# Rebuilding 64-bit weights from rows that are loaded one byte late, and products of zeros in TensorE's modelled idle time

## The chip, the cores and the metric

The kernel runs on one core of a Trainium2 chip. The metric is the time of one execution on the device in microseconds (us); three runs of the kernel before took 1581.19 to 1584.06 us, median 1582.57. The engines of a core run side by side and wait for each other by semaphores: TensorE (PE; PEld is its weight load), VectorE (DVE), ScalarE (ACT), GpSimd (POOL) and SyncE (SP), whose queue issues all the DMAs here. Each engine takes its instructions in program order.

## The reference

Three layers over 8 sequences of 576 tokens (4608 tokens, 512 features): a landmark attention (8 heads of 64), a layer with a Fourier mix, a normalization and two matrices, and a gated layer with three matrices.

```python
A, Bm, C = sm(q, k_lm), sm(q_lm, k_lm), sm(q_lm, k)      # softmaxes; 32 landmarks
Z = Bm.T / (norm1(Bm) * norminf(Bm) + 1e-06)
for _ in range(6):
    Z = 2 * Z - Z @ Bm @ Z
x = heads_to_features(A @ Z @ C @ v)                      # 8 x 576 x 512
u = x + real(fft(fft(x, axis=1), axis=2))
un = (u - mean(u)) / sqrt(var(u) + 1e-06)
x = u + relu(un @ w_ch1) @ w_ch2                          # 512 x 2048, 2048 x 512
xk, xr = mu_k * x + (1 - mu_k) * x_prev, mu_r * x + (1 - mu_r) * x_prev
k = relu(xk @ w_k)                                        # 512 x 1024
out = sigmoid(xr @ w_r) * ((k * k) @ w_v)                 # 512 x 512, 1024 x 512
```

The five matrices arrive as 64-bit floats. The kernel makes a 32-bit float of each value and splits it in two 16-bit floats, high and low part; a product of two matrices is then three matmuls (high by high, high by low, low by high).

## The kernel before, in words

**Stages.** `phase1` does the attention and the Fourier mix of one sequence (batch) at a time, in 32-bit floats, and adds its result to blocks `ub` of 512 tokens. `norm` normalizes such a block: sums by matmuls with a column of ones (`one`), three Newton steps on small tiles, then the two halves `un`. `block_a` multiplies it with w_ch1 and w_ch2: 16 steps `first(f)` (12 matmuls into a bank `ph`, then Relu on ACT and the low part on DVE) and 16 steps `second(f)` (12 matmuls into the four banks `acc`), 384 matmuls of 128x512 for a block. There are nine blocks; after the last comes the gated layer (`Gated`), 280 us behind the start and later mostly matmuls back to back. The matmuls of `block_a` and `Gated` form one chain in fixed order.

**Weights.** `Weights.run` handles a piece of 128x512 weights: 32 pieces of w_ch1 and w_ch2 (in the order four of w_ch1, four of w_ch2, four times), then 20 pieces of the gated layer, whose halves go back to memory. A piece is loaded as pairs of 32-bit words (512 KB) into one of three rooms in turn (`wst` twice, `more`; the last eight of the 32 pieces use `wst` alone). Then come three ACT passes (Square, Sign and Copy make a mask of the exponent), three DVE passes on integers (shifts, and, or), an ACT pass for the high half (`w1h`, `w2h`) and a DVE pass for the low half (`w1l`, `w2l`). The room is free for the next load when the low half is done. `first(0)` needs the first four pieces, `second(f)` the f-th of w_ch2.

**What sets the order.** All operations are recorded first; `Plan.issue` is a list scheduler that gives each engine its order by modelled costs: an operation can stand as soon as its inputs' modelled ends plus HOP (0.2) have passed, and among those ready the one with the highest key (longest way to the end, plus a lead: NOW for the chain, START for the first batch, SOON for the others, CONVERT for weights) goes first. Weight operations get a further margin `slack` on each edge from another engine or a DMA, 1.5 in the kernel before. A DMA is modelled with its bytes / 340e3 plus 2.0. PSUM has eight banks: `acc` holds 0 to 3, `ph` 4 and 5, and banks from `gp()` take any that are free, all eight as long as the chain hasn't begun.

**Names.** Line 180 is the helper that issues every operation of DVE, ACT and POOL, L308 every DMA, L323 every matmul, L336 every transpose by TensorE; groups are told apart by tile names. `kbd`, `qbd`: landmarks of keys and queries; `RX`, `bdR`: the six steps of the series for Z; `Ae`, `Ao`, `acs`: the Fourier tables' products; `tmp`: squares for the variance; `small`: the Newton steps; `h`: the inner activations.

Of the kernel before, what the change touches and what calls it, by code (L numbers as in the profile page):

```python
# [11 lines left out]
F32 = mybir.dt.float32  # L12
F16 = mybir.dt.float16
I32 = mybir.dt.int32
AF = mybir.ActivationFunctionType
ALU = mybir.AluOpType
AX = mybir.AxisListType
# [13 lines left out]
WCH = 512  # L31
# [96 lines left out]
class Op:  # L128
    def __init__(self, index, eng, run, cost, port=False, nbytes=0):
        self.index, self.eng, self.run, self.cost = index, eng, run, cost  # L130
        self.port, self.nbytes = port, nbytes
        self.preds, self.succs = set(), []
        self.tail = self.lead = self.est = self.end = 0.0
        self.group = self.last = None

NOW, START, CONVERT, SOON = 1000.0, 400.0, 170.0, 200.0


class Engine:
# [44 lines left out]
class Plan:  # L187
# [6 lines left out]
    def __init__(self, nc, shadow):  # L194
        self.nc, self.shadow = nc, shadow
        self.ops, self.groups = [], []
        self.slots, self.turn = {}, {}
        self.lead = self.slack = 0.0
        self.chained, self.count = None, 0
        self.v = Engine(self, nc.vector, "v")  # L200
        self.s = Engine(self, nc.scalar, "s")
        self.g = Engine(self, nc.gpsimd, "g")
# [112 lines left out]
    def mm(self, out, lhsT, rhs, start, stop, chain=False, **kw):  # L315

        cost = wide(rhs) / 2400.0 + 0.0025
        if rhs.dtype == F32:
            cost = max(4 * cost, 0.17)
        share = 4 if wide(lhsT) <= 32 else 2 if wide(lhsT) <= 64 else 1  # L320

        def run():
            self.nc.tensor.matmul(  # L323
                out.real(), lhsT=lhsT.real(), rhs=rhs.real(), start=start, stop=stop, **kw
            )

        op = self.record("pe", run, cost / share, [out], [lhsT, rhs])
        if chain:
            op.lead = 0.0
            if self.chained:  # L330
                op.preds.add(self.chained)
            self.chained = op

    def tr(self, out, in_, ident):
        def run():
# [29 lines left out]
    def issue(self):  # L365
        ops = self.ops
# [17 lines left out]
        avail = {e: [] for e in free}  # L384
        pending, order = [], []
        bank = {n: 0.0 for n in range(8)}
        fixed, holds = set(), {}
        port = dma = 0.0

        def ready(op):  # L390
            op.est = max(
# [48 lines left out]
        for op in ops:  # L440
            if not op.preds:
                ready(op)
        while len(order) < sum(op.eng is not None for op in ops):
            when = []
            for e in free:
                if avail[e]:
                    when.append((free[e], e))
                elif later[e]:
                    when.append((max(free[e], later[e][0][0]), e))
            g = grant()  # L450
            if g and (not when or g[0] <= min(when)[0]):
                t, op, got = g
                pending.remove(op)
                for x, b in zip(op.group, got):
                    x.bank, x.left = b, len(x.ops)
# [10 lines left out]
            start = max(t, port) if op.port else t  # L466
            free[e] = end = start + op.cost
# [5 lines left out]
            op.begin = start  # L473
            order.append(op)
            done(op, end)
        self.order, self.span = order, max(op.end for op in order)
        for op in order:
            op.run()
# [18 lines left out]
class Weights:  # L497


    KEEP = float(np.int32(0x3FFFFFFF).view(np.float32))  # L500

    def __init__(self, iss, pool):
        self.iss, self.pool = iss, pool

    def run(self, src, hi, lo, room=None):


        iss = self.iss
        v_, s_ = iss.v, iss.s
        st, bits = room or (  # L510
            iss.tile(self.pool, [128, WCH, 2], I32, "wst", bufs=2),
            iss.tile(self.pool, [128, WCH], I32, "wbits", bufs=2),
        )
        iss.load(st.rearrange("p f w -> p (f w)"), src)
        low, high = st[:, :, 0], st[:, :, 1]


        w = bits.bitcast(F32)
        s_.activation(bits, high.bitcast(F32), AF.Square, scale=256.0)
        s_.activation(w, bits, AF.Sign)  # L520
        s_.activation(w, w, AF.Copy, scale=self.KEEP)
        v_.scalar_tensor_tensor(
            bits, high, 3, bits, op0=ALU.logical_shift_left, op1=ALU.bitwise_and
        )
        v_.scalar_tensor_tensor(
            bits, low, 29, bits, op0=ALU.logical_shift_right, op1=ALU.bitwise_or
        )
        v_.scalar_tensor_tensor(
            bits, high, -0x40000000, bits, op0=ALU.bitwise_and, op1=ALU.bitwise_or
        )  # L530
        dram = None
        if hi is None:
            dram = lo
            both = st.rearrange("p f w -> p (f w)")[:, 0:WCH].bitcast(F16).rearrange(
                "p (x f) -> p x f", x=2
            )
# [419 lines left out]
def build(nc, tc, a):  # L956
# [5 lines left out]
    with stack, tc.manual_schedule():  # L962
# [30 lines left out]
        one = iss.tile(com, [128, 1], F32, "one")  # L993
        v_.memset(one, 1.0 / DM)
        ones = one.to_broadcast([128, 128])
        w1 = [iss.tile(pa, [128, 4, FF1], F16, f"w1{x}") for x in "hl"]
        w2 = [iss.tile(pa, [128, 16, DM], F16, f"w2{x}") for x in "hl"]
        weights = Weights(iss, com)
# [128 lines left out]
        def block_a(i, un):  # L1127
            u = ub[i]
            acc = acc_banks()
            hs = {}  # L1130
            iss.lead = NOW

            def first(f):
                ps = ph()
                sl = slice(128 * f, 128 * f + 128)
                for c in range(4):
                    for n, (x, y) in enumerate(PARTS):
                        mm(
                            ps, w1[x][:, c, sl], un[c][y], c == 0 and n == 0,
                            c == 3 and n == 2, chain=True,  # L1140
                        )
                h = hs[f] = iss.tile(com, [128, 2, 512], F16, "h", bufs=3)
                s_.activation(h[:, 0], ps, AF.Relu)
                v_.scalar_tensor_tensor(
                    h[:, 1], ps, 0.0, h[:, 0], op0=ALU.max, op1=ALU.subtract
                )

            def second(f):
                h = hs.pop(f)
                for m in range(4):  # L1150
                    sl = slice(128 * m, 128 * m + 128)
                    for n, (x, y) in enumerate(PARTS):
                        mm(
                            acc[m], w2[x][:, f, sl], h[:, y], f == 0 and n == 0,
                            f == 15 and n == 2, chain=True,
                        )

            first(0)
# [10 lines left out]

        more = iss.place(pa, [128, 4 * BLK], I32, "more", "ub_2")  # L1170
        rooms = [None, None, (
            more[:, 0:2 * WCH].rearrange("p (f w) -> p f w", w=2), more[:, 2 * WCH:3 * WCH]
        )]
        iss.lead, iss.slack = CONVERT, 1.5
        for n, x in enumerate(w12_items):
            weights.run(*x, room=rooms[n % 3] if n < 24 else None)
        iss.lead = 0.0
# [247 lines left out]
```

## Time and profile before

| | |
|---|---|
| median of three runs | 1582.57 us |
| profiled execution: time, span | 1584.5 us, 1582.7 us |
| busy over the span | PE 1529.7, DVE 883.9, ACT 600.5, POOL 288.4 us |
| granted TensorE clock, mean | 0.978 of full |
| DVE: 156 integer passes on weights (132 + 24) | 94.4 + 16.8 us |

The busy time of PE adds up matmuls whose ends are modelled; the granted clock (PEclk) says what share of 2.4 GHz the chip allowed, 0.50 being 1.2 GHz. Rows of a timeline or of groups name the operation as out<-in with sizes; "x40" counts records, and a 32-bit matmul leaves two of them.

### The profile page before, as it was taken

How to read it: one execution, taken by the hardware profiler on the slowest of the kernel's cores; microseconds unless marked ns; L12 is line 12 of the kernel's file. 1: busy time of each engine (PE TensorE's matmuls, PEld its weight loads, DVE VectorE, ACT ScalarE, POOL GpSimd, SP SyncE). 2: the span in 40 equal slices, each digit the busy share in tenths (PEclk: the TensorE clock that was granted, in tenths of full speed). 3: DMA queues.
4: the chain of work that ended last, by engine and by line, in shares of the span. 5: the costliest groups of instructions: out<-in, count | busy, mean ns of one | idle time of the engine just before them, and what ended most of it. 6: DMA issues, size and time to landing. Idle time of an engine off the chain costs nothing.

```text
span 1582.7 us, 20918 instructions
## 1 busy us (share of the span) xinstructions
PE 1529.7 (97%) x8182; PEld 784.4 (50%) x8182; DVE 883.9 (56%) x1802; ACT 600.5 (38%) x1233; POOL 288.4 (18%) x347
## 2 busy tenths in 40 slices
PE   6879899999999999999999999999999999999998
PEld 5535455555564554554544444444444444444443
DVE  6798887776764764634515344211587766643222
ACT  4465654444433433322312123111655544443221
POOL 2012020221210210210102012000454533221100
PEclk8788899999999999999999999999999999999999
DMA  7243414132322222100002200000121011000000
GB/s 272 67 133 121 134 55 152 38 115 76 100 71 81 86 72 80 61 1 28 1 0 80 107 28 0 27 0 28 53 80 54 27 54 54 28 1 27 27 28 27
DMA packets 43587, 97.87 MB, mean 62 GB/s; under 512 B 4064, under 2 KB 9440, under 8 KB 42976
## 3 DMA queue, kind: packets, MB, share of 16 engines
q1 hardware_dynamic: 43488, 96.53, 17.8%
q8 instruction: 65, 1.06, 0.3%
q14 instruction: 34, 0.28, 0.1%
HBM read 72.39 MB, written 24.12 MB: 61 GB/s over the span
## 4 chain that ended last, share of the span: by engine, by line
PE 93%; DVE 4%; ACT 1%; issue 1%; DMA 0%; SPq 0%; POOL 0%; ACTq 0%; DVEq 0%
PE ph L323 35%; PE acc L323 35%; PE gp L323 21%; PE gp L336 2%; DVE wbits L180 1%; DVE more L180 0%; DVE small L180 0%; DMA k<-in_k 0%; DVE uc L180 0%; DVE w1l L180 0%; DVE h L180 0%; ACT h L180 0%; DVE d L180 0%; DVE un L180 0%; DVE w2l L180 0%
## 5 line engine op out<-in xcount | busy, mean ns | idle before, releaser
L323 PE MATMUL ph<-un,w1h 128*128 128x512 f16 x1152 | 353.6, 382 | 10.6 <-DVE bst L180 6.1
L323 PE MATMUL acc<-h,w2h 128*128 128x512 f16 x1152 | 350.8, 382 | 1.2 <-ACT w2h L180 1.2
L180 DVE SCALAR_TENSOR_TENSOR h<-ph,h 128x512 f16<-128x512 f32 x144 | 99.3, 690 | 283.2 <-ACT h L180 282.4
L180 ACT ACTIVATE h<-ph 128x512 f16<-128x512 f32 x144 | 85.9, 597 | 379.2 <-PE ph L323 378.7
L323 PE MATMUL acc<-h,w2l 128*128 128x512 f16 x576 | 219.8, 382 | 4.3 <-DVE w2l L180 4.3
L323 PE MATMUL ph<-un,w1l 128*128 128x512 f16 x576 | 219.8, 382 | 3.1 <-DVE w1l L180 3.1
L323 PE MATMUL ph<-xk,w_k 128*128 128x512 f16 x864 | 199.6, 379 | 0.0
L323 PE MATMUL acc<-w_v,k 128*128 128x512 f16 x864 | 198.9, 379 | 0.0
L323 PEld LDWEIGHTS <-w1h 128*128 128x128 f16 x1152 | 113.0, 99 | 138.4 <-issue 14.5
L323 PEld LDWEIGHTS <-w2h 128*128 128x128 f16 x1152 | 113.6, 99 | 131.6 <-issue 8.8
L180 DVE TENSOR_TENSOR rk<-rk 128x512 f32<-128x512 f32 x72 | 55.5, 770 | 146.3 <-ACT rk L180 145.9
L323 PEld LDWEIGHTS <-k 128*128 128x128 f16 x864 | 84.6, 98 | 100.6
L323 PEld LDWEIGHTS <-w_k 128*128 128x128 f16 x864 | 84.5, 98 | 99.7
L323 PE MATMUL gp<-w_r,xr 128*128 128x512 f16 x432 | 99.3, 379 | 0.7 <-ACT rs L180 0.7
L180 DVE SCALAR_TENSOR_TENSOR wbits<-wst,wbits 128x512 int32<-128x512 int32 x132 | 94.4, 731 | 2.8 <-ACT wbits L180 1.6
L180 ACT ACTIVATE rk<-ph 128x512 f32<-128x512 f32 x72 | 43.0, 597 | 129.2 <-PE ph L323 121.6
L323 PEld LDWEIGHTS <-w2l 128*128 128x128 f16 x576 | 57.1, 99 | 69.9 <-DVE w2l L180 5.3
L323 PEld LDWEIGHTS <-w1l 128*128 128x128 f16 x576 | 57.1, 99 | 68.6 <-DVE w1l L180 4.6
L180 DVE TENSOR_TENSOR k<-rk,k 128x512 f16<-128x512 f32 x72 | 59.3, 823 | 29.3 <-ACT k L180 29.1
L180 POOL TENSOR_TENSOR sq<-sq 128x513 f32<-128x513 f32 x27 | 36.6, 1356 | 198.7 <-ACT sq L180 198.1
L180 POOL TENSOR_TENSOR xr<-xt,xr 128x512 f16<-128x512 f32 x36 | 48.6, 1375 | 112.1 <-ACT xr L180 112.0
L323 PEld LDWEIGHTS <-xr 128*128 128x128 f16 x432 | 42.2, 98 | 51.4 <-issue 0.9
(156 smaller groups left out, 1977.3 us busy)
## 6 DMA issues: line engine op xcount, KB each, us to landing
wst<-in_w_ch SPq DMA_DIRECT2D x24, 512.0 KB, 4.0
q<-in_q SPq DMA_DIRECT2D x16, 578.0 KB, 5.1
k<-in_k SPq DMA_DIRECT2D x16, 576.0 KB, 4.6
ys<-ub SPq DMA_DIRECT2D x36, 256.0 KB, 2.1
out<-o SPq DMA_DIRECT2D x36, 256.0 KB, 2.0
yb<-ys SPq DMA_DIRECT2D x8, 1026.0 KB, 5.3
v<-in_v SPq DMA_DIRECT2D x8, 1024.0 KB, 5.6
more<-in_w_ch SPq DMA_DIRECT2D x8, 512.0 KB, 4.4
```

What stands on the lines that cost most here:

```text
L180: f(real(out), *map(real, args), **{k: real(x) for k, x in kw.items()})
L323: self.nc.tensor.matmul(out.real(), lhsT=lhsT.real(), rhs=rhs.real(), start=start, stop=stop, **kw)
L336: self.nc.tensor.transpose(out.real(), in_.real(), ident.real())
```

## The change

**The load.** A row of 512 values (4096 bytes) is written to its room from byte 1 on, so that a value's top byte (sign and upper exponent bits) lies alone at the start of the next word pair and the following four bytes of interest form one aligned word. Two Prelu on ACT turn the signed top byte into the top byte of the 32-bit float and write it into `top`, a tile that was set to zero once; one DVE pass shifts the word right by 5 and ors `top` in, in place. The high and low halves then read that word with a stride of 8 bytes. The pieces of the gated layer use one `top` (the other's place holds their halves).

**Products of zeros.** Where the planner's model leaves TensorE idle, `issue` puts int((idle - 0.15) / 0.3) matmuls of a zero tile (128x128 by 128x512) in front of the next matmul: before the chain into bank 3, which no other tile then uses, and inside a block's chain into `acc[3]`, adding zero. There are 102 of them: 28 in front of the first matmul, 89 ahead of the chain's first, 13 later in the first block.

**The margin.** `slack` for weight operations goes from 1.5 to 0.6.

```diff
-    KEEP = float(np.int32(0x3FFFFFFF).view(np.float32))
+    EDGE, STEEP = 56.125, 1024.0
...
-        iss.load(st.rearrange("p f w -> p (f w)"), src)
-        low, high = st[:, :, 0], st[:, :, 1]
-        w = bits.bitcast(F32)
-        s_.activation(bits, high.bitcast(F32), AF.Square, scale=256.0)
-        s_.activation(w, bits, AF.Sign)
-        s_.activation(w, w, AF.Copy, scale=self.KEEP)
+        iss.load(st.bitcast(U8)[:, 1:8 * WCH + 1], src.bitcast(U8))
+        def words(dt, at):
+            return st.bitcast(dt)[:, at:2 * WCH + at].rearrange("p (f w) -> p f w", w=2)[:, :, 0]
+        x = words(F32, 2)
+        byte = st.bitcast(I8)[:, 8:8 * WCH + 8].rearrange("p (f b) -> p f b", b=8)[:, :, 0]
+        s_.activation(x, byte, AF.Prelu, bias=self.EDGE, alpha=self.STEEP)
+        s_.activation(
+            top.bitcast(I8).rearrange("p (f b) -> p f b", b=4)[:, :, 3], x, AF.Prelu,
+            scale=8.0, bias=-8.0 * (56.0 + self.EDGE), alpha=1.0 / self.STEEP,
+        )
         v_.scalar_tensor_tensor(
-            bits, high, 3, bits, op0=ALU.logical_shift_left, op1=ALU.bitwise_and
+            words(I32, 1), words(I32, 1), 5, top,
+            op0=ALU.logical_shift_right, op1=ALU.bitwise_or,
         )
-        v_.scalar_tensor_tensor(
-            bits, low, 29, bits, op0=ALU.logical_shift_right, op1=ALU.bitwise_or
-        )
-        v_.scalar_tensor_tensor(
-            bits, high, -0x40000000, bits, op0=ALU.bitwise_and, op1=ALU.bitwise_or
-        )
+        w = words(F32, 1)
...
-        fixed, holds = set(), {}
+        fixed, holds = {WARM}, {}
...
+            if e == "pe" and (not warming or warming[-1] is not None):
+                into = warming[-1] if warming else None
+                idle = start - max(was, self.warm_from.end)
+                order += [
+                    Op(0, "warm", partial(self.warm, into), 0.0)
+                ] * int((idle - 0.15) / 0.3)
...
+            z = zero.real()[:, 0:1]
+            nc.tensor.matmul(
+                into.real() if into else spare[0], lhsT=z.to_broadcast([128, 128]),
+                rhs=z.to_broadcast([128, 512]), start=not into, stop=not into,
+            )
...
-        iss.lead, iss.slack = CONVERT, 1.5
+        iss.lead, iss.slack = CONVERT, 0.6
```

DVE at the end of the first batch's series, where the first pieces are converted (`wbits`, `more`, `wst`: rooms and masks; `bdY`: end of the series; `ks`, `qs`: the second batch's landmarks). Before:

```order
L180 TENSOR_TENSOR RX1_305<-gp_441,RX1_305 128x64
L180 SCALAR_TENSOR_TENSOR wbits_272<-wst_108,wbits_272 128x512
L180 SCALAR_TENSOR_TENSOR bdY_465<-gp_452,bst_187,c_mask4_92 128x256 x2
...
L180 SCALAR_TENSOR_TENSOR wbits_312<-wst_110,wbits_312 128x512 x3
L180 SCALAR_TENSOR_TENSOR more_112<-more_112 128x512 x3
L180 SCALAR_TENSOR_TENSOR w1l_529<-wbits_272,w1h_505 128x512
L180 TENSOR_REDUCE ks_534<-k_176 128x32
```

The same place now:

```order
L186 TENSOR_TENSOR RX1_349<-gp_495,RX1_349 128x64
L186 SCALAR_TENSOR_TENSOR w1l_505<-wst_116,w1h_476 128x512
L186 SCALAR_TENSOR_TENSOR bdY_518<-gp_507,bst_223,c_mask4_100 128x256 x2
L186 SCALAR_TENSOR_TENSOR wst_118<-wst_118,wtop_84 128x512
L186 SCALAR_TENSOR_TENSOR more_86<-more_86 128x512
L186 TENSOR_REDUCE ks_549<-k_212 128x32 x3
L186 SCALAR_TENSOR_TENSOR w1l_505<-wst_118,w1h_476 128x512
```

Three integer passes for a piece have become one, the first low half stands ahead of `bdY` rather than behind three pieces' passes, and the second batch's landmarks follow sooner.

PE at the chain's first matmul (`ph`), behind the first block's variance (`one`,`tmp`) and the transposes that spread its result (`ident`,`small`). Before:

```order
L323 MATMUL gp_629<-one_80,tmp_627 128x1 x4
L323 MATMUL gp_629<-one_80,tmp_638 128x1 x4
L336 MATMUL gp_677<-ident_90,small_661 128x128 x4
L323 LDWEIGHTS w1h_505
L323 MATMUL ph_706<-un_687,w1h_505 128x512
```

The same place now (`E_747` is the second batch's; of the 11 products of zeros in front of the chain one is shown, and one of the 6 in front of the transposes of `E_747`):

```order
L330 MATMUL gp_798<-one_82,tmp_808 128x1 x4
L346 MATMUL gp_843<-ident_98,E_747 128x128
...
L1043 LDWEIGHTS zero_88
L1043 MATMUL spare_125<-zero_88 128x512
...
L346 MATMUL gp_843<-ident_98,E_747 128x128 x3
...
L346 MATMUL gp_868<-ident_98,small_837 128x128 x4
...
L330 LDWEIGHTS w1h_476
L330 MATMUL ph_903<-un_883,w1h_476 128x512
```

46 matmuls of the second batch's attention, and the products of zeros, now stand ahead of the chain's first matmul (247 others instead of 201).

ACT around the same place (`un`: high halves of the normalized block; `h`: first inner activation). Before:

```order
L180 ACTIVATE un_694<-uc_620 128x512
L180 ACTIVATE wbits_698<-wst_659 128x512
L180 ACTIVATE wbits_698<-wbits_698 128x512 x2
L180 ACTIVATE un_708<-uc_623 128x512
L180 ACTIVATE h_728<-ph_706 128x512
```

The same place now:

```order
L186 ACTIVATE un_888<-uc_786 128x512
L186 ACTIVATE un_905<-uc_794 128x512
L186 ACTIVATE w1h_476<-wst_759 128x512
L186 ACTIVATE wst_877<-wst_877 128x512
L186 ACTIVATE wtop_84<-wst_877 128x512
L186 ACTIVATE h_931<-ph_903 128x512
```

The four high halves stand together; weight passes of the ninth and later pieces lie between them and `h`.

## Rows read from the trace of the kernel before

**Rows 1.** The page: span of the profiled execution.
```profile
span 1582.7 us, 20918 instructions
```

**Rows 2.** Five stretches: stretch, length, then busy us and instructions by engine.
```profile
core 0: us, PE busy (x) PEld busy (x) DVE busy (x) ACT busy (x) POOL busy (x), PEclk, DMA share, GB/s
0.00:82.20 82.20, 59.41 (x336) 43.87 (x337) 56.35 (x147) 37.78 (x91) 10.69 (x19) 0.77 0.47 163
82.20:120.00 37.80, 28.18 (x157) 14.41 (x157) 34.55 (x67) 22.26 (x41) 4.57 (x5) 0.91 0.47 148
120.00:280.00 160.00, 146.60 (x897) 80.75 (x898) 126.08 (x284) 87.63 (x200) 23.02 (x29) 0.93 0.34 112
280.00:1574.00 1294.00, 1291.54 (x6776) 643.78 (x6775) 664.15 (x1303) 452.86 (x905) 250.08 (x294) 1.00 0.13 46
1574.00:1582.70 8.70, 3.94 (x19) 1.57 (x16) 2.82 (x4) 0.00 (x0) 0.00 (x0) 0.85 0.32 121
```

**Rows 3.** Order of time on PE: start, length, what, idle before and its releaser.
```profile
9.07 6.80 PE L323 MATMUL gp<-kbd,q 128*97 128x64 f32 x40 [9.07 <-POOL kbd L180]
...
67.45 6.46 PE L323 MATMUL gp<-one,tmp 128*128 128x1 f32 x32 [1.52 <-ACT tmp L180]
...
82.22 1.01 PE L323 MATMUL ph<-un,w1h 128*128 128x512 f16 x2 [4.47 <-ACT wbits L180]
83.03 0.63 PE L323 MATMUL ph<-un,w1l 128*128 128x512 f16 x1
83.46 1.06 PE L323 MATMUL ph<-un,w1h 128*128 128x512 f16 x2
...
89.25 0.38 PE L323 MATMUL acc<-h,w2l 128*128 128x512 f16 x1
89.47 0.59 PE L323 MATMUL acc<-h,w2h 128*128 128x512 f16 x2
...
93.78 2.88 PE L323 MATMUL gp<-kbd,q 128*97 128x64 f32 x32
...
224.84 3.63 PE L323 MATMUL gp<-one,tmp 128*128 128x1 f32 x32
```

**Rows 4.** A stretch of the first batch, same columns as Rows 2.
```profile
24.00:52.00 28.00, 24.73 (x181) 18.22 (x179) 20.82 (x65) 14.96 (x43) 8.73 (x13) 0.58 0.42 142
```

**Rows 5.** SP in order of time: loads into the room `more`.
```profile
88.98 0.33 SPq L308 DMA_DIRECT2D more<-in_w_ch  x1
...
179.90 0.34 SPq L308 DMA_DIRECT2D more<-in_w_ch  x1
```

**Rows 6.** Groups by shape: busy us, mean ns, idle before and its releaser.
```profile
L180 DVE SCALAR_TENSOR_TENSOR wbits<-wst,wbits 128x512 int32<-128x512 int32 x132 | 94.4, 731 | 2.8 <-ACT wbits L180 1.6
L180 ACT ACTIVATE wbits<-wst 128x512 int32<-128x512 f32 x44 | 29.2, 663 | 1.8 <-DVE w2l L180 1.4 <-ACT w2h L180 0.4
L180 ACT ACTIVATE wbits<-wbits 128x512 f32<-128x512 int32 x44 | 27.5, 627 | 0.9
L180 POOL TENSOR_TENSOR tmp<-tmp 128x512 f32<-128x512 f32 x21 | 27.2, 1295 | 74.4 <-ACT tmp L180 73.9
L180 POOL MEMSET xt<- 128x1 f32 x64 | 5.1, 98 | 29.1 <-ACT xt L180 29.0
```

**Rows 7.** Instructions on the tile `wst` by stretch: DVE busy, ACT busy, clock, DMA.
```profile
82.20:120.00 37.80, 12.79 (x18) 3.32 (x5) 0.91 0.47 148
120.00:280.00 160.00, 37.32 (x50) 11.22 (x17) 0.93 0.34 112
```

**Rows 8.** DMA issues: count, KB each, median us from issue to landing.
```profile
wst<-in_w_ch SPq DMA_DIRECT2D x24, 512.0 KB, 4.0
ys<-ub SPq DMA_DIRECT2D x36, 256.0 KB, 2.1
yb<-ys SPq DMA_DIRECT2D x8, 1026.0 KB, 5.3
v<-in_v SPq DMA_DIRECT2D x8, 1024.0 KB, 5.6
```

More of the change, by code (lines that the diff above doesn't have):

```diff
@@ L14 @@
 I32 = mybir.dt.int32
+I8 = mybir.dt.int8
+U8 = mybir.dt.uint8
 AF = mybir.ActivationFunctionType
@@ L133, in __init__ @@
         self.tail = self.lead = self.est = self.end = 0.0
-        self.group = self.last = None
+        self.group = self.last = self.opens = self.closes = None
 NOW, START, CONVERT, SOON = 1000.0, 400.0, 170.0, 200.0
+WARM = 3
 class Engine:
@@ L199, in __init__ @@
         self.chained, self.count = None, 0
+        self.warm = None
         self.v = Engine(self, nc.vector, "v")
@@ L331, in mm @@
                 op.preds.add(self.chained)
+            else:
+                self.first_chained = op
             self.chained = op
+        return op
     def tr(self, out, in_, ident):
@@ L386, in issue @@
         bank = {n: 0.0 for n in range(8)}
-        fixed, holds = set(), {}
+        fixed, holds = {WARM}, {}
         port = dma = 0.0
+        warming = []
         def ready(op):
@@ L442, in issue @@
                 ready(op)
-        while len(order) < sum(op.eng is not None for op in ops):
+        while any(avail.values()) or any(later.values()) or pending:
             when = []
@@ L466, in issue @@
             start = max(t, port) if op.port else t
+            was = free[e]
             free[e] = end = start + op.cost
@@ L473, in issue @@
             op.begin = start
+            if e == "pe" and (not warming or warming[-1] is not None):
[4 more added lines that the diff above has]
+                ] * int((idle - 0.15) / 0.3)
+            if op is self.first_chained:
+                warming.append(None)
+            if op.opens is not None:
+                warming.append(op.opens)
+            if op.closes:
+                warming.append(None)
             order.append(op)
             done(op, end)
+        assert all(not n for n in left.values())
         self.order, self.span = order, max(op.end for op in order)
@@ L497, with clear @@
 class Weights:
-    KEEP = float(np.int32(0x3FFFFFFF).view(np.float32))
+    EDGE, STEEP = 56.125, 1024.0
     def __init__(self, iss, pool):
         self.iss, self.pool = iss, pool
+        self.tops = [self.clear(iss.tile(pool, [128, WCH], I32, "wtop", f"wtop{n}")) for n in range(2)]
+        self.count = 0
+    def clear(self, x):
+        self.iss.g.memset(x, 0)
+        return x
     def run(self, src, hi, lo, room=None):
@@ L509, in run @@
         v_, s_ = iss.v, iss.s
-        st, bits = room or (
-            iss.tile(self.pool, [128, WCH, 2], I32, "wst", bufs=2),
-            iss.tile(self.pool, [128, WCH], I32, "wbits", bufs=2),
-        )
-        iss.load(st.rearrange("p f w -> p (f w)"), src)
-        low, high = st[:, :, 0], st[:, :, 1]
-        w = bits.bitcast(F32)
-        s_.activation(bits, high.bitcast(F32), AF.Square, scale=256.0)
-        s_.activation(w, bits, AF.Sign)
-        s_.activation(w, w, AF.Copy, scale=self.KEEP)
-        v_.scalar_tensor_tensor(
-            bits, high, 3, bits, op0=ALU.logical_shift_left, op1=ALU.bitwise_and
+        if room is None:
+            st = iss.tile(self.pool, [128, 2 * WCH + 2], I32, "wst", bufs=2)
+            top = self.tops[self.count % 2 if hi is not None else 0]
+            self.count += 1
+        else:
+            st, top = room
+        iss.load(st.bitcast(U8)[:, 1:8 * WCH + 1], src.bitcast(U8))
[7 more added lines that the diff above has]
+            scale=8.0, bias=-8.0 * (56.0 + self.EDGE), alpha=1.0 / self.STEEP,
         )
         v_.scalar_tensor_tensor(
-            bits, low, 29, bits, op0=ALU.logical_shift_right, op1=ALU.bitwise_or
-        )
-        v_.scalar_tensor_tensor(
-            bits, high, -0x40000000, bits, op0=ALU.bitwise_and, op1=ALU.bitwise_or
-        )
+            words(I32, 1), words(I32, 1), 5, top,
+            op0=ALU.logical_shift_right, op1=ALU.bitwise_or,
+        )
+        w = words(F32, 1)
         dram = None
@@ L533, in run @@
             dram = lo
-            both = st.rearrange("p f w -> p (f w)")[:, 0:WCH].bitcast(F16).rearrange(
-                "p (x f) -> p x f", x=2
-            )
+            both = iss.tile(self.pool, [128, 2, WCH], F16, "wboth", "wtop1")
             hi, lo = both[:, 0], both[:, 1]
@@ L995, in build, with warm @@
         ones = one.to_broadcast([128, 128])
+        zero = iss.tile(com, [128, 2], F16, "zero")
+        iss.lead = NOW
+        iss.warm_from = g_.memset(zero, 0.0)
+        iss.lead = START
+        spare = []
+        def warm(into):
+            if not spare:
+                spare.append(ps_pool.get().tile(
+                    [128, 512], F32, tag=f"bank{WARM}", name="spare", bufs=1
+                ))
+            z = zero.real()[:, 0:1]
[3 more added lines that the diff above has]
+            )
+        iss.warm = warm
         w1 = [iss.tile(pa, [128, 4, FF1], F16, f"w1{x}") for x in "hl"]
@@ L1152, in second @@
                     for n, (x, y) in enumerate(PARTS):
-                        mm(
+                        op = mm(
                             acc[m], w2[x][:, f, sl], h[:, y], f == 0 and n == 0,
@@ L1156, in second @@
                         )
+                        if m == 3 and f == 0 and n == 0:
+                            op.opens = acc[3]
+                        if m == 3 and f == 15 and n == 1:
+                            op.closes = True
             first(0)
@@ L1171, in build @@
         rooms = [None, None, (
-            more[:, 0:2 * WCH].rearrange("p (f w) -> p f w", w=2), more[:, 2 * WCH:3 * WCH]
+            more[:, 0:2 * WCH + 2], weights.clear(more[:, 2 * WCH + 2:3 * WCH + 2])
         )]
-        iss.lead, iss.slack = CONVERT, 1.5
+        iss.lead, iss.slack = CONVERT, 0.6
         for n, x in enumerate(w12_items):
```

## Prediction

> **What bounds the kernel now.** I read the table of stretches first. The span is 1582.7 us [rows 1]; the execution took 1584.5 us, 1.8 outside the span and 1.9 above the median of the three runs. From 280 to 1574 us TensorE is busy for 1291.54 of 1294 us at clock 1.00 [rows 2]: nothing in the change can shorten that stretch, only start it sooner. What can be gained lies before 280 us and has two parts. First, idle time of PE: 82.2 - 59.41 = 22.8 us before the chain's first matmul, 37.8 - 28.18 = 9.6 us up to 120, 160 - 146.6 = 13.4 us up to 280. Second, work at the lower clock level: busy time by (1 - granted clock) is 59.41 x 0.23 = 13.7, 28.18 x 0.09 = 2.5 and 146.6 x 0.07 = 10.3 us.
>
> The clock rows are not the whole of it. In the first 20 us the clock is shown as 1.00, but 40 records of kbd,q take 6.80 us (0.17 each) and 32 of the same form later 2.88 us (0.09 each) [rows 3]: PE also runs at half rate there. So about 72 us of the first 280 are lost, 9.1 of them before the first operands exist (idle until 9.07 [rows 3]).
>
> Then DVE. It is busy 34.55 of 37.8 us right after the chain begins [rows 2]. Passes that name the room `wst` are 12.79 us of that stretch and 37.32 us of the next [rows 7], so the stretch in which PE starves is the one in which DVE converts weights. Last the queue of loads: the room `more` is loaded at 88.98 and 179.90 us and four times between [rows 5], five rounds of 18.2 us. Three rooms turn together, so a piece of weights comes every 6.1 us. A step of the chain (12 + 12 matmuls at 0.22 us, 89.25 to 89.47 [rows 3]) takes 5.2 us and wants two pieces. Hence the round of the rooms bounds the first block, and PE fills the rest with the second batch as far as it can.
>
> **Part 1, the passes.** Per piece two of three integer passes on DVE go, 2 x 0.73 = 1.46 us, and one of three ACT passes, 0.63 us [rows 6]. Over 52 pieces that is 76 us of DVE and 33 of ACT, but 20 of these pieces fall in a time when PE is full, so they give nothing. The new passes read or write with a stride. The trace has a strided read of 8 bytes at 663 ns and the contiguous pass at 627 [rows 6]; no row has bytes written at a stride of 4. The Prelu passes lie between 0.60 and 1.3 us (twice the row); I take 0.66 from the strided row. Prelu brings no table switch: both programs load an activation table twice.
>
> **Part 2, the margin.** A piece crosses to another engine or the queue five times in a round of the new form (load, ACT, DVE, ACT, DVE, next load), and each planned crossing shrinks by 0.9. So the round goes from 18.2 to 18.2 - 1.46 - 0.63 - 4.5 = 11.6 us, 3.9 us a piece: above the 2.6 us that a pure chain wants, but below the 6.0 us that PE's own work between 82.2 and 280 leaves for each of 27 pieces (28.18 + 146.6 - 12.8 of low clock = 162 us; 27 because four w1l and one w2l are done by then). So PE is mostly no longer starved. Of its 23.0 us idle and 12.8 us low clock after 82.2 I take back two thirds, 24 us; bounds 10 (DVE and ACT stand in order behind weights as now) and 33.
>
> **Part 3, the load at byte 1.** No row shows a transfer shifted by one byte. The nearest is yb, whose rows are 2052 bytes long and so start off any power of two: 1026 KB land in 5.3 us, v's 1024 KB in aligned rows in 5.6 [rows 8]. So I take 0. Bounds: 0.3 us faster (the difference of these two rows), and as slow as twice the bytes, 5.6 instead of 4.0 us.
>
> The Trainium skill, "DMA: Bandwidth & Descriptors", section on how a descriptor splits into AXI transactions, says that a piece of memory which doesn't start on a 256-byte boundary costs an extra transaction. Counted for the write side that is an estimate of 17 instead of 16 for a row of 4096 bytes, about 0.25 us a load and some 2 us over nine rounds; the sum would then be 1549. The yb row shows no such cost.
>
> **Part 4, the products of zeros.** 28 stand in front of the first matmul, behind three clearings of 512 columns on POOL (between 0.1 us, a clearing of one column, and 1.3 us, a sum of 512 columns [rows 6]; I take 0.5). At the lower level one costs 0.43 us (83.03 to 83.46), at the higher 0.22 [rows 3]. Begun at half rate, the chain runs at full rate at 89 us at the latest; I take 8 at 0.43 and 20 at 0.22, bounded by all at one or the other: from about 2.5 to 10.3 us, 1.2 us later than 9.07. The 40 kbd,q records then gain 40 x 0.08 = 3.2 us. Net 1.5 us gained; bounds -5 (all 28 at 0.43, begun at 4) and +3.
>
> The Trainium skill, "TensorE: Matmul & The Clock Gate", Part 1, calls the throttled state the default, which activity releases. By the clock rows, 1.00 from the start, the 28 products would buy nothing and the sum be about 3 us worse; the two durations of kbd,q agree with the page.
>
> From 24 to 52 us PE is busy 24.73 of 28 us at clock 0.58 [rows 4]: at full clock that is 10.4 us less work. Chains through DVE, ACT and POOL (3.3 us idle there already) keep some; I take 7, bounds 3 and 10. In the first block's normalization one,tmp takes 6.46 us where the same 32 records later take 3.63 [rows 3]: 2.8 us. The 4.47 us wait at 82.22 ends with weight passes on ACT that now stand behind all of `un`; I take 1.7 of it (three passes of 0.64 stood there), bounds 0 and 3. Sum before the chain: 1.5 + 7 + 2.8 + 1.7 = 13 us, so its first matmul comes near 69 us.
>
> Cost: 11 products of zeros stand in the first batch's tail and 13 in the first block; where PE has no idle time they cost 24 x 0.22 = 5.3 us. I take 2; the other 50 ahead of the chain lie in waits of its 22.8 idle us.
>
> **Sum.** 1582.7 - 13 - 24 + 2 = 1547.7 us span, 1549.5 for an execution like the profiled one, 1547.6 by the median of the runs. Forecast 1547, its own range 1536 to 1558.
>
> **Rivals.**
> 1. *Starvation ends altogether.* All of 35.8 us after 82.2, and 17 ahead of it: 1582.6 - 53 = 1530. For it: DVE loses about 50 x 2/3 passes between 120 and 280 and is then busy some 100 of 160 us. Against: the second batch needs DVE and ACT in the same time, and orders with less margin break sooner. 0.20.
> 2. *Only the clock pays.* The order of before stood on a margin of 1.5; with 0.6 the engines wait in order for weights as often as now, and of Part 2 only some 5 us of clock remain: 1582.6 - 13 - 5 + 2 = 1567. For it: the planner models an ACT pass at 0.61, strided ones take 0.66. 0.16.
> 3. *Zeros don't raise the clock,* so part of the change does not do what it says: without the 28's gain, the 7 and the 2.8 us, and with products at 0.43 (some 5 us over the idle time), 1547 + 11 + 5 = 1563. No row shows PE on zeros; for the forecast speaks that from 280 to 1574 us, whatever the shapes, the clock is 1.00 [rows 2]. 0.10.
> 4. *Slower: late landings hold ACT.* The first Prelu stands at the earliest 4.3 us behind its load in the model (1.5 + 2.0 + 0.2 + 0.6), the median landing is 4.0 us [rows 8]. If bytes at an odd address land as late as 1 MB does (5.6), ACT stands 1.3 us at each of 32 pieces, `h` behind it, `second(f)` behind `h`, PE behind that: 42 us, 1547 + 42 = 1589. It decides from a landing of 5.4 us on (35 / 32 = 1.1 us a piece, none covered). Against: the yb row, and the chain's 2.6 us of the next `first` as cover. 0.06.
>
> **How the numbers follow.** Forecast 0.48, rivals 0.20, 0.16, 0.10, 0.06. The range reaches down past rival 1 and up past rival 2: 1526 to 1570, leaving out rival 4 and the ends. Under 0.2% (3.2 us) a measurement cannot tell a change; faster by more 0.91, no change 0.03, slower 0.06.
>
> **What would show it.** Clock 1.00 from about 8 us on and kbd,q records near 0.09 us; the chain's first matmul at 65 to 73 us; `more` loaded every 11 to 13 us; PE idle between the chain's begin and 280 us near 8 us instead of 23; the same 1294 us of full PE work behind. Wrong it would be if the loads land past 5 us, the Prelu passes take over 1 us, or DVE and ACT rows show waits for weights in front of `h`.

## The result, and the profile after

The changed kernel takes 1536.47 us (median of four runs, 1535.23 to 1539.29) against 1581.88 us for the kernel before (four runs of the same session, 1580.83 to 1584.06): a ratio of 0.9714, 95% interval 0.9696 to 0.9731, or 45.4 us less. The forecast was 1547 with a range of 1526 to 1570: direction and range hold, the median lies 10.5 us under the forecast, between it and rival 1 (1530). The span of the profiled execution is 1534.9 us, 47.8 less than before [rows 1].

The table of stretches of the kernel after, cut as before [rows 2]; columns are the stretch, its length, busy us of each engine (instructions), then the granted clock, DMA share and GB/s:

```profile
core 0: us, PE busy (x) PEld busy (x) DVE busy (x) ACT busy (x) POOL busy (x), PEclk, DMA share, GB/s
0.00:82.20 82.20, 77.03 (x529) 48.05 (x530) 65.91 (x169) 46.22 (x110) 14.19 (x25) 0.98 0.61 214
82.20:120.00 37.80, 37.80 (x284) 22.19 (x282) 30.53 (x83) 22.59 (x51) 10.28 (x13) 1.00 0.42 136
120.00:280.00 160.00, 159.66 (x940) 89.16 (x940) 116.65 (x275) 86.46 (x185) 30.52 (x37) 0.99 0.38 119
280.00:1574.00 1294.00, 1247.70 (x6537) 618.36 (x6534) 604.86 (x1174) 422.98 (x836) 232.25 (x276) 1.00 0.12 43
```

Between 82.2 and 280 us TensorE now idles for 0.3 us (23.0 before) and the clock stays up but for 3.4 us. Behind 280 us stands the same kind of work, only less of it (1247.7 instead of 1291.5 us), since it began sooner. Nearly all of the gain, 47.0 of 47.8 us, is made in the first 340 us: VectorE adds the last matrix of the second block to `ub` from 337.4 us on, before from 384.4.

The beginning and the first normalization on TensorE, in order of time (start, length, operation, count, idle before and what ended it), to compare with [rows 3]:

```profile
2.27 7.72 PE L1043 MATMUL spare<-zero 128*128 128x512 f16 x28 [2.27 <-POOL zero L186]
9.83 3.56 PE L330 MATMUL gp<-kbd,q 128*97 128x64 f32 x40
13.33 2.21 PE L330 MATMUL gp<-k,qbd 128*64 128x288 f32 x14
...
45.14 0.47 PE L330 MATMUL gp<-kbd,q 128*97 128x64 f32 x4
...
53.13 2.15 PE L330 MATMUL gp<-k,qbd 128*64 128x288 f32 x14
...
66.89 4.00 PE L330 MATMUL gp<-one,tmp 128*128 128x1 f32 x32
...
71.21 2.60 PE L1043 MATMUL spare<-zero 128*128 128x512 f16 x6
...
74.08 0.60 PE L346 MATMUL gp<-ident,small 128*128 128x128 f32 x4
74.52 2.57 PE L1043 MATMUL spare<-zero 128*128 128x512 f16 x11
77.34 0.89 PE L330 MATMUL ph<-un,w1h 128*128 128x512 f16 x2 [0.26 <-DVE uc L186]
```

The 28 products of zeros take 7.72 us (8 x 0.43 + 20 x 0.216 = 7.76), and the 40 records behind them 3.56 us, 0.09 each, where the same 40 took 6.80 before. The half rate of before went on behind them, to some 20 us; the 14 records of `k,qbd`, 2.21 us here, took 4.16:

```profile
15.79 4.16 PE L323 MATMUL gp<-k,qbd 128*64 128x288 f32 x14
```

The chain's first matmul stands at 77.34 us (82.22 before), behind 82 records of the second batch (48 of `kbd,q`, 16 of `k,qbd`, 8 of `ks,qbd`, 10 of `E`; the first at 45.14, since GpSimd writes that batch's `kbd` at 42.0). They take some 8.7 us, and the kernel before did none of them by then.

The groups of the new passes (busy us, mean ns, idle before and its releaser), to compare with [rows 6]:

```profile
L186 ACT ACTIVATE wtop<-wst 128x512 int8<-128x512 f32 x44 | 34.4, 781 | 0.9
L186 ACT ACTIVATE wst<-wst 128x512 f32<-128x512 int8 x44 | 29.6, 672 | 5.3 <-DMA wst<-in_w_ch 3.2 <-DMA wst<-in_w_k 1.4 <-DMA wst<-in_w_v 0.6
L186 DVE SCALAR_TENSOR_TENSOR wst<-wst,wtop 128x512 int32<-128x512 int32 x44 | 32.7, 743 | 3.1 <-ACT wtop L186 3.1
L186 DVE SCALAR_TENSOR_TENSOR w1l<-wst,w1h 128x512 f16<-128x512 f32 x12 | 9.1, 757 | 1.4 <-ACT w1h L186 1.4
```

The mean of a group on VectorE hides two kinds of pass. The median is 683 ns for the shift-and-or and 682 for `w1l`; before it was 683 both for an integer pass and for `w1l`. Of the 104 integer passes and low halves now, the 76 with at most 0.1 us of GpSimd work beside them took 705 ns at most; the 12 over 800 ns all ran beside GpSimd, as this one did:

```profile
97.65 0.92 POOL L186 TENSOR_TENSOR Ao<-d,Ao 97x256 f16<-97x256 f32 x1 [0.92 <-ACT Ao L186]
97.95 1.16 DVE L186 SCALAR_TENSOR_TENSOR w2l<-wst,w2h 128x512 f16<-128x512 f32 x1
```

And the DMA issues (count, KB each, median us to landing), to compare with [rows 8]:

```profile
wst<-in_w_ch SPq DMA_DIRECT2D x24, 512.0 KB, 3.9
yb<-ys SPq DMA_DIRECT2D x8, 1026.0 KB, 5.1
v<-in_v SPq DMA_DIRECT2D x8, 1024.0 KB, 5.9
```

In these 24 loads into `wst` bytes at an odd address land in 3.9 us, aligned rows took 4.0; the loads into `more` took 4.6 (4.4 before), those of `w_k` 5.0 (4.3). What TensorE still waits for, the longest four of eight rows over the whole span (engine, for whom, us in all, times, longest):

```profile
PE spare L1043 <- POOL zero L186: 2.3, 1, 2.3
PE gp L346 <- DVE small L186: 1.1, 2, 0.6
PE gp L330 <- ACT Ae L186: 0.9, 1, 0.9
PE gp L330 <- DVE RX L186: 0.7, 2, 0.5
```

No wait for a piece of weights is left among them.

### The profile page after: what moved, and what is told of

It reads as the page before. It is cut to its first block, busy times and chain, and to the rows that moved or that the text cites. A ratio compares the mean times of both kernels' runs of the same rounds, so it can differ in the third digit from the quotient of the medians.

```text
span 1534.9 us, 20950 instructions
## 1 busy us (share of the span) xinstructions
PE 1522.2 (99%) x8284; PEld 777.8 (51%) x8284; DVE 818.0 (53%) x1698; ACT 578.2 (38%) x1181; POOL 287.2 (19%) x351
## 4 chain that ended last, share of the span: by engine, by line
PE 96%; DMA 1%; DVE 1%; ACT 1%; issue 0%; SPq 0%; POOL 0%; ACTq 0%; DVEq 0%
PE ph L330 37%; PE acc L330 36%; PE gp L330 21%; PE gp L346 2%; DMA ident<-in_ident 1%; DMA wst<-in_w_ch 0%; DVE small L186 0%; PE spare L1043 0%; SPq L315 0%; DVE uc L186 0%; DMA out<-o 0%; DVE d L186 0%; ACT d L186 0%; ACT wtop L186 0%; DVE o L186 0%
## 5 line engine op out<-in xcount | busy, mean ns | idle before, releaser
L330 PE MATMUL ph<-un,w1h 128*128 128x512 f16 x1152 | 349.9, 379 | 0.4 <-DVE uc L186 0.3
L186 DVE TENSOR_TENSOR xt<-xt,rs 128x512 f32<-128x512 f32 x72 | 60.5, 869 | 2.9 <-ACT rs L186 2.8
```

What stands on the lines that cost most here:

```text
L186: f(real(out), *map(real, args), **{k: real(x) for k, x in kw.items()})
L330: self.nc.tensor.matmul(out.real(), lhsT=lhsT.real(), rhs=rhs.real(), start=start, stop=stop, **kw)
```

## The experiments

Twelve kernels were run; the kernel before measured 1582.99, 1581.45 and 1582.27 us beside the three groups of four. "Clock loss" below is the sum, over windows of 2 us up to 400 us, of TensorE's busy time by (1 - granted clock).

### Each part with and without the others

```diff
 # no_zeros
-            if e == "pe" and (not warming or warming[-1] is not None):
+            if False:
-        fixed, holds = {WARM}, {}
+        fixed, holds = set(), {}
 # margin_15
-        iss.lead, iss.slack = CONVERT, 0.6
+        iss.lead, iss.slack = CONVERT, 1.5
 # old_passes: Weights and its load as before; margin 0.6 and zeros stay
 # zeros_alone: old_passes and margin_15; passes_alone: no_zeros and margin_15
 # margin_alone: old_passes and no_zeros
```

`no_zeros`. 

> New passes and margin 0.6, no products of zeros, bank 3 free again as before. Theory (the round of the rooms starves PE after the chain's begin, low clock costs about a quarter of the gain): 1548 to 1553, PE idle between the first chain product and the end of the second block still below 8 us, clock 0.50 again between 24 and 52 us. Rival (the clock is the main thing; passes and margin matter little): 1562 or more. Second rival (the zeros only fill time that is idle anyway and the cold stretches are hidden behind DVE): within 3 us of the changed kernel, 1536 to 1540.

Measured 1551.67 us, ratio 0.981 (0.9784 to 0.9836): as my theory had it, the zeros are worth 15.2 us beside the other two parts.

`margin_15`. 

> The changed kernel with the margin put back to 1.5. Theory (planned crossings set the round of the rooms): five crossings of 0.9 come back, the round grows by up to 4.5 us, 1542 to 1550. Rival (only the passes' work on DVE counts, the margin is immaterial): 1536 to 1539. Second rival (the larger margin matches the real landing better, so engines wait less): 1533 to 1536.

Measured 1558.4 us, ratio 0.9854 (0.983 to 0.9879). Not as expected: the margin is worth 21.9 us.

`old_passes`. 

> The three ACT and three DVE passes of before, aligned load, with margin 0.6 and products of zeros. Theory (a round without 4.5 us of margin, but with 2.1 us more work per piece, DVE over 85% busy in the first block): 1548 to 1558. Rival (DVE's load alone starves PE): 1565 or more. Second rival (margin alone did it): 1536 to 1540.

Measured 1567.9 us, ratio 0.9912 (0.9887 to 0.9937), as the rival had it: the passes are worth 31.4 us.

`zeros_alone`. 

> The kernel before with products of zeros alone (old passes, margin 1.5; 204 products). Theory: the front gains about 10 us by the clock, the starvation after the chain's begin stays: 1568 to 1574. Rival (the clock is the main thing): 1555 or less. Second rival (the products, most of them in the first block, cost as much as they give): 1578 to 1584.

Measured 1561.74 us, ratio 0.9879 (0.9849 to 0.9908). Faster than expected, and 6 us faster than with the smaller margin added.

So the three single values are 15.2 + 21.9 + 31.4 = 68.5 us where the change gives 45.4. The two missing combinations:

`passes_alone`. 

> The changed kernel with the margin back at 1.5 and without the products of zeros: only the new passes and the load at byte 1 stand against the kernel before. It would finish the eight combinations of the three parts. My theory, from the first four runs: the parts are not additive. The smaller margin pays because the passes have left VectorE and ScalarE the room for the earlier unpacking, and the passes pay because the smaller margin lets that room be used. By it the passes alone give little: the new passes gave 3.3 us beside the zeros with the margin at 1.5 (1561.7 to 1558.4), so 1572 to 1580 us here, and the idle of TensorE stays above 40 us. Rival, that the parts add up: the zeros are worth 15.2 us and the margin 21.9 us in the changed kernel, so this run would stand at the changed kernel's 1522 + 15 + 22 us above the common start, that is between 1552 and 1562 us, with an idle near 30 us.

Measured 1569.69 us, ratio 0.9924 (0.9909 to 0.9939): 2 us under the theory's range and 8 over the additive one's, with 40.0 us of idle time. The passes alone give 12 us.

`margin_alone`. 

> The kernel before with only the margin changed from 1.5 to 0.6: old passes, no products of zeros. My theory: the old passes need all of VectorE and ScalarE in the second batch's loading, so an order that unpacks earlier finds no room and gives nothing or costs a little, 1578 to 1590 us, as the margin beside the old passes and the zeros cost 6 us (1561.7 to 1567.9). Rival, that the parts add up: the margin's 21.9 us are had here too, 1558 to 1564 us. A third: half of it, because the zeros of the other pair stood in the way of the margin's gain, 1568 to 1575 us.

Measured 1584.63 us, ratio 1.0023 (1.0011 to 1.0035): as the theory had it, the smaller margin by itself costs 3 us.

| us | margin 1.5 | margin 0.6 | the margin gives |
|---|---|---|---|
| old passes, no zeros | 1582 (before) | 1584.6 | +3 |
| old passes, zeros | 1561.7 | 1567.9 | +6 |
| new passes, no zeros | 1569.7 | 1551.7 | -18 |
| new passes, zeros | 1558.4 | 1536.5 | -22 |

The margin changes sign with the passes. Every edit makes the planner set the whole order anew, and that alone can move the time: margins of 1.2 and 0.3 both stand 11 us above 0.6 (below). Beside that the +3 and +6 are small; the distance of 21 and 28 us between old and new passes is not. Where TensorE starves in `margin_alone`, VectorE has no time left; four stretches of it, columns as above:

```profile
64.00:72.00 8.00, 3.91 (x32) 3.83 (x32) 7.18 (x24) 7.70 (x14) 0.00 (x0) 0.80 0.29 102
72.00:80.00 8.00, 3.44 (x10) 1.60 (x11) 7.97 (x14) 3.63 (x6) 0.00 (x0) 0.50 0.09 22
104.00:112.00 8.00, 4.14 (x31) 2.81 (x31) 7.83 (x19) 4.78 (x10) 1.81 (x2) 0.86 0.38 114
112.00:120.00 8.00, 4.49 (x14) 2.17 (x14) 7.53 (x21) 3.75 (x6) 1.34 (x2) 0.50 0.67 233
```

TensorE is busy for 16.0 of these 32 us, VectorE for 30.5. An order that wants the pieces earlier finds VectorE full there.

The account of the profiled executions, from the spans, TensorE's busy time and the count of zeros (0.216 us each, and 1.7 us more for the eight at the lower level):

| | span | PE idle | clock loss | zeros | remaining work |
|---|---|---|---|---|---|
| before | 1582.7 | 53.0 | 27.3 | 0 | 1502.4 |
| margin_alone | 1580.9 | 54.9 | 25.1 | 0 | 1500.9 |
| passes_alone | 1568.0 | 40.0 | 26.1 | 0 | 1501.9 |
| no_zeros | 1551.5 | 33.9 | 17.4 | 0 | 1500.2 |
| zeros_alone | 1560.0 | 13.3 | 3.4 | 45.8 (204) | 1497.5 |
| old_passes | 1563.9 | 21.5 | 4.9 | 39.9 (177) | 1497.6 |
| margin_15 | 1556.6 | 18.9 | 4.6 | 33.2 (146) | 1499.9 |
| after | 1534.9 | 12.7 | 3.4 | 23.7 (102) | 1495.0 |

The last column agrees within 8 us, and the four without zeros carry 4 to 5 us of half-rate work in the first 20 us (`kbd,q` and `k,qbd`) that the clock rows show as 1.00; without it they stand at 1495 to 1497 us. So the time is TensorE's own work of 1495 to 1500 us plus what it idles, what the clock takes and what it spends on zeros. The zeros bring clock and idle time down everywhere, but where TensorE starves as before they fill the starvation (204 of them, 45.8 us) without ending it. The passes with the margin end most of it without any zeros: from 82 to 400 us TensorE idles for 6.1 us in `no_zeros`, for 23.3 in the kernel before.

### Whose room the smaller margin needs

```diff
 # dve_again, on no_zeros: behind the shift-and-or of a piece
+        for _ in range(2):
+            v_.scalar_tensor_tensor(
+                words(I32, 1), words(I32, 1), 0, words(I32, 1),
+                op0=ALU.logical_shift_right, op1=ALU.bitwise_or,
+            )
 # act_again, on no_zeros: the second Prelu of a piece twice
+        for _ in range(2):
             s_.activation(
```

`dve_again`. 

> The changed kernel without the products of zeros (1551.7 us), in which VectorE does two further passes of 0.74 us on each piece behind the shift-and-or (a word or-ed with itself), so that a piece costs VectorE what it did before the change, while ScalarE keeps the two Prelu. Theory: the smaller margin pays only where VectorE has the room that the passes left (the smaller margin alone measured 1584.6, the new passes alone 1569.7, both 1551.7), so the gain goes as far as VectorE carries it: 1575 to 1590 us, with VectorE busy over 125 of the 160 us between 120 and 280 and TensorE idle over 45 us in the whole span. Rival: the room that counts is ScalarE's, or the number of crossings between engines, which is the same here as in the changed kernel: 1551 to 1560 us.

Measured 1578.65 us, ratio 0.9981 (0.9971 to 0.999), 27.0 us above `no_zeros`: the theory's range, and most of the 33 us that the passes give at this margin (1584.6 to 1551.7). The trace kept of it is of an execution of 7496 us, far from the nine others (1577.05 to 1581.09), so the two rows that the theory named can't be read.

`act_again`. 

> The changed kernel without the products of zeros (1551.7 us), in which ScalarE does its second Prelu twice on each piece, 0.78 us more, so that a piece costs ScalarE a little more than before the change. Theory of VectorE's room: ScalarE is busy 86 of 160 us between 120 and 280 and has time left, so 1551 to 1558 us. Rival of ScalarE's room: the smaller margin's 18 us go and the time is 1565 us or more.

Measured 1552.99 us, ratio 0.9818 (0.9801 to 0.9834), 1.3 us above `no_zeros`, though ScalarE is much busier between 120 and 280 us (86.37 us in `no_zeros`):

```profile
120.00:280.00 160.00, 159.92 (x954) 91.82 (x952) 112.67 (x263) 101.23 (x207) 28.60 (x36) 0.99 0.37 116
```

So two integer passes of VectorE for a piece are worth 27 us at the smaller margin, and a further pass on ScalarE next to nothing. That a longer way through the piece (1.5 us against 0.8) rather than VectorE's time does it was not separated; by length alone `act_again` would have lost some 14 us.

### Which products of zeros pay

```diff
 # first_28
-            if e == "pe" and (not warming or warming[-1] is not None):
+            if e == "pe" and not was:
 # long_gaps
-                order += [
-                    Op(0, "warm", partial(self.warm, into), 0.0)
-                ] * int((idle - 0.15) / 0.3)
+                count = int((idle - 0.15) / 0.3)
+                if count >= 5:
+                    order += [Op(0, "warm", partial(self.warm, into), 0.0)] * count
```

`first_28`. 

> The changed kernel with the products of zeros at the very start alone; those of later gaps left out. The prediction gave the 28 at the start a net of 1.5 us (3.2 won at kbd,q, 1.2 us later begun, bounds -5 and +3), so 1551.7 - 1.5 = 1550 us (1547 to 1553), and the clock falls to 0.5 again between 24 and 52 us. Rival, that a clock once raised stays up as long as TensorE is kept nearly busy by its own work: most of the 15.2 us of the zeros are had by the first 28, 1538 to 1543 us.

Measured 1544.73 us, ratio 0.9768 (0.9754 to 0.9783): 6.9 us of the zeros' 15.2 come with the first 28, between the two expectations; the clock does fall again (0.50 from 26 to 42 us). That a bank is set aside for the zeros, which `no_zeros` gives back, may be part of it; that was not tried.

`long_gaps`. 

> The changed kernel with products of zeros only where the order has five or more in one gap: 69 of them in place of 102, the 28 at the start kept. Theory that each short row of zeros stands on TensorE's path by its own length, since TensorE waits for almost nothing else after the start: 33 products of 0.216 us are 7.1 us, so 1529 to 1533 us. Rival one: the short rows stood in waits that come back as idle, 1535 to 1538 us and the idle of TensorE 5 to 7 us above the 12.7 of the changed kernel. Rival two: the clock falls again where they are gone, in 64 to 84 us and 170 to 190 us, 1540 us or more, with a granted clock under 0.7 in one of these stretches.

Measured 1541.04 us, ratio 0.9743 (0.9729 to 0.9758): 4.6 us slower with 33 zeros fewer: the time of the second rival. The clock falls, but mainly in a stretch that it had not named: its mean is 0.51 from 33 to 40 us (1.00 in the kernel after), 0.83 from 64 to 84 (0.91) and 0.91 from 170 to 190 (0.91). The same Fourier products in `long_gaps`, where 13 zeros between 27.7 and 34 us are left out, and then in the kernel after (order of time on TensorE):

```profile
37.81 0.45 PE L330 MATMUL gp<-c_cosT,Ae 96*128 96x289 f16 x1
38.05 0.45 PE L330 MATMUL gp<-c_sinT,Ao 96*128 96x289 f16 x1
...
40.31 0.28 PE L330 MATMUL gp<-c_sinT,Ao 96*128 96x289 f16 x1
40.43 0.27 PE L346 MATMUL gp<-ident,bdY 128*128 128x128 f32 x1
```

```profile
36.46 0.29 PE L330 MATMUL gp<-c_cosT,Ae 96*128 96x289 f16 x1
36.58 0.29 PE L330 MATMUL gp<-c_sinT,Ao 96*128 96x289 f16 x1
...
37.91 0.28 PE L330 MATMUL gp<-c_sinT,Ao 96*128 96x289 f16 x1
38.03 0.27 PE L346 MATMUL gp<-ident,bdY 128*128 128x128 f32 x1
```

They follow each other every 0.24 us there and every 0.12 us here. Over the span, `long_gaps` saves 7.1 us of zeros and pays 4.4 us of idle time (17.1 against 12.7) and 5.0 us of clock (8.4 against 3.4).

### The size of the margin

```diff
-        iss.lead, iss.slack = CONVERT, 0.6
+        iss.lead, iss.slack = CONVERT, 1.2      # margin_12; margin_03: 0.3
```

`margin_12`. 

> The changed kernel with the margin at 1.2 in place of 0.6 (1.5 was run, 1558.4 us). Theory that the margin works in proportion, each unit of it holding a piece back for its share: 21.9 us over 0.9 is 24 us for a unit, so 1536.5 + 14.6 = 1551 us (1547 to 1555). Rival, that one decision of the order tips somewhere between 0.6 and 1.5: the time is near one of the two ends, under 1541 or over 1556 us. Which it is shows in the time at which the second block of the scores ends (337.4 us with 0.6) and in the distance of the loads of the second batch.

Measured 1547.26 us, ratio 0.9785 (0.9769 to 0.9801), at the lower edge of the proportional theory: 10.8 of the 21.9 us are lost with two thirds of the margin. The second block ends at 344.7 us (337.4 with 0.6, 358.8 with 1.5), and `more` is loaded every 16.4 us (15.1 and 16.5).

`margin_03`. 

> The changed kernel with the margin at 0.3 in place of 0.6. The margins 1.5, 1.2 and 0.6 measured 1558.4, 1547.3 and 1536.5 us, 37 us for a unit from 1.5 to 1.2 and 18 from 1.2 to 0.6. Theory that it flattens, since behind the chain's first matmul TensorE's idle time is down to 0.8 us and an earlier piece can end no wait: 1533 to 1539 us. Rival: landings and passes longer than modelled now hold the engines in program order, 1541 us or more, with waits for the DMAs of `wst` and `more` over 8 us on ScalarE (3.2 us and 3.1 us in the changed kernel).

Measured 1547.3 us, ratio 0.9782 (0.9768 to 0.9797): 10.8 us slower than 0.6. That is the rival's time, but not for its reason: ScalarE waits 4.3 us for the loads of `wst` that the nine blocks use and not at all for `more` (3.2 and 3.1 us in the kernel after). The large loss is one knot between 84 and 101 us. In order, a stretch of all engines, then TensorE, ScalarE and VectorE there:

```profile
88.00:92.00 4.00, 3.09 (x8) 0.91 (x6) 0.73 (x2) 0.88 (x2) 0.00 (x0) 0.67 0.96 335
```

```profile
86.11 1.03 PE L330 MATMUL ph<-un,w1h 128*128 128x512 f16 x2
...
94.61 1.17 PE L330 MATMUL gp<-RX,bdR 128*128 128x96 f32 x4 [3.52 <-DVE RX L186]
```

```profile
91.12 0.60 ACT L186 ACTIVATE h<-ph 128x512 f16<-128x512 f32 x1 [3.56 <-PE ph L330]
```

```profile
91.75 0.69 DVE L186 SCALAR_TENSOR_TENSOR h<-ph,h 128x512 f16<-128x512 f32 x1 [3.27 <-ACT h L186]
92.36 0.40 DVE L186 SCALAR_TENSOR_TENSOR RX<-gp,bst,c_eye 128x32 f32<-128x32 f32 x2
```

TensorE runs at the lower level (two matmuls in 1.03 us), so `ph` is late, `h` waits on ScalarE and VectorE, and `RX` of the second batch, which stands behind `h` on VectorE, holds TensorE for 3.5 us. The granted clock, at 1.00 again from 91 to 94 us, is back at 0.50 behind that wait. From 82 to 102 us 6.4 us go by the clock and 3.9 by idle time, in the kernel after none. No version tried beats the changed kernel.

## Why the prediction was right, and where its sizes were off

**The account.** Ahead of the chain I forecast 13 us, behind it 24, for the zeros' cost 2. Measured, in the two profiles: the chain begins 4.9 us sooner (82.22 to 77.34) with 8.7 us of the second batch already done, 13.6 us for 13. Behind 82.2 us, idle time fell from 23.0 to 0.3 us and clock loss from 12.8 to 1.7 us, 33.8 us in all; 13 zeros stand there for 2.8 us. The step that failed is the "two thirds" of Part 2: 24 us of 35.8, where 33.8 came back. That difference of 9.8 us is nearly all of the 10.5 us by which the forecast was too high. These terms make 44.6 of the 47.8 us; where the other 3 come from stays open. Rival 1's mechanism, that starvation ends altogether, holds behind the chain's begin; of the 17 us that it wanted ahead of it 13.6 came.

**Part 1.** Costs per piece were close on VectorE: integer passes and low halves together take 1.37 us less for a piece, where 1.46 was forecast from the mean of 731 ns (the median is 683). On ScalarE 672 + 781 replace 663 + 627 + 626 ns, and a high half, reading at a stride of 8 bytes, takes some 660 for 620: 0.42 us saved and not the 0.60 that two passes of 0.66 would leave. Both Prelu lie within their bounds. What Part 1 did not say is that the passes are the condition of Part 2: alone they give 12 us, with the margin 33 (1584.6 to 1551.7).

**Part 2.** I let passes and margin shorten one round independently, 18.2 to 11.6 us, of which the margin 4.5. The table of eight refutes that: the margin alone costs 3 us. And the round is not 11.6 us; SP issues the loads of `more` at these times in the kernel after, the first and the last of five:

```profile
84.15 0.33 SPq L315 DMA_DIRECT2D more<-in_w_ch  x1
...
144.53 0.33 SPq L315 DMA_DIRECT2D more<-in_w_ch  x1
```

Four rounds of 15.1 us on the mean (12.4 to 21.2), 5.0 us a piece. That is under the 6.0 us which the prediction had worked out as TensorE's need: the conclusion stood on the comparison with 6.0, not on 11.6, and that it held is in part luck. For the round alone does not set the starvation: at 16.4 to 16.5 us a round, idle time and zeros from 82 to 400 us are 11.6 us in `margin_12`, 17.6 in `passes_alone` and 22.3 in `margin_15`. What does set it, beside VectorE's time, was not separated.

**Part 3** holds for the loads into `wst`: 3.9 us. The Trainium skill's extra transaction ("DMA: Bandwidth & Descriptors", section on how a descriptor splits into AXI transactions), an estimate of 0.25 us a load, does not show in this landing time. The Trainium skill tells it of bytes that are fetched; to count it for the write side was my own step. The later landings of `w_k` (5.0 us for 4.3) can't decide it, since kernels with aligned rows scatter as much: 3.8 in `margin_alone`, 4.7 in `zeros_alone`. Rival 4 falls: ScalarE waits 3.2 us in all for the loads of `wst` that the nine blocks use, and 3.1 for `more`.

**Part 4.** The first 28 went as worked out (7.72 us, clock up, 0.09 us a record), and rival 3 falls: zeros raise the clock. That work in the throttled state comes first and activity releases it ("TensorE: Matmul & The Clock Gate", Part 1, of the Trainium skill) agrees with 0.17 us a record without and 0.09 us behind the zeros. The net for the 28 was summed wrongly: 3.2 us won less 1.2 of delay are 2.0, not 1.5. And it counted only `kbd,q`, while the half rate of before went on over `k,qbd` (4.16 us, 2.21 after), a loss that the 72 us at the prediction's start leave out too. Measured, the first 28 give 6.9 us; all zeros together give 15.2 where their terms in Part 4 less their cost made 9. `one`,`tmp` took 4.00 us, not 3.63, since the clock is at 0.50 from 70 to 73.5 us in spite of the zeros.

**What would show it.** Right: the clock from 8 us (but for two stretches of 3.4 us, at 70 and 179 us), the `kbd`,`q` records, the full work behind. Wrong: the chain's first matmul (77.3, not 65 to 73), because the second batch's 8.7 us in front of it stood in the order and I had not added them; less these it is 68.7, where 69 was worked out. Wrong too: the distance of `more` (15.1, not 11 to 13) and the idle time up to 280 us (0.3, not 8). Rival 2 falls: without zeros the new passes and the margin measure 1551.7 us, 31 us less than before.

## What to carry to other kernels

Where a scheduler's margin and an engine's load meet, neither has a value of its own: the same smaller margin measured +3 us with VectorE full and -18 us with two passes a piece gone, so look in the starved stretch for the engine that is busy for all of it, and free that first. A busy TensorE says nothing while it multiplies zeros: subtract those, and add idle time and clock loss, and the kernels compare. Filler work paid here in short gaps too: without the 33 zeros that stood fewer than five to a gap the kernel lost 4.6 us. Read a group's median beside its mean: 74 ns that look like the price of a stride were two of twelve passes that ran beside GpSimd.

## What the runs showed of the hardware that was not expected

- An ACT pass that writes bytes at a stride of 4 takes 781 ns for 128x512, where the pass that reads bytes at a stride of 8 and writes floats at a stride of 8 takes 672.
- Reading 32-bit words at a stride of 8 bytes costs ScalarE some 40 ns in a high half (median of the gated layer's 20: 662 ns, 621 for adjacent words) and VectorE nothing in a low half (median 682 against 683).
- VectorE's passes on weights take up to 1.77 us beside GpSimd's work, and at most 0.71 us where 0.1 us or less of it runs beside them.
- In the first 20 us without zeros the clock rows show 1.00 while the records run at half rate (0.17 us for 0.09): there the durations tell the clock, and the row does not.
